# A 1 KB read at the head of a DMA queue, and a new order of the first loads, in a fused attention and gated-MLP kernel

## The chip, the cores and the metric

The kernel runs on one core of one Trainium2 chip. The metric is the device time of one execution in microseconds (us). All timed runs here count as fast (undisturbed) runs. One execution of each kernel was also profiled, and its trace is what the views below show. A trace has its own span, from the first to the last instruction, about 1.7 us shorter than the device time.

In the profile PE is TensorE's matmuls, PEld its weight loads, DVE the vector engine, ACT the scalar engine, POOL GpSimd and SP SyncE. A name with "q" (SPq, ACTq) is the engine's sequencer, which issues DMAs.

## The reference, cut to what matters

One token sequence of 2048 rows and 640 columns is layer-normalized and goes through two branches, which are added to the input.

```python
xn = _layernorm(x, axis=-1)
return x + _A_ref(xn, A_wqkv, A_w_phi, A_wo) + _B_ref(xn, B_w1, B_w3, B_w2)
# _A_ref: q, k, v = xn @ wqkv, 32 heads of 20; feature maps, linear attention; @ wo
# _B_ref: (silu(xn @ w1) * (xn @ w3)) @ w2, with 1536 hidden columns
```

All inputs are bf16. Only the opening matters here: row tiles of 128 rows of x are normalized, transposed on TensorE and multiplied by the value weights wv, the last 640 columns of wqkv. wv comes in five slices of 128 rows (160 KB each), because the product runs over 640 = 5 x 128.

## The kernel before

The opening issues ten small reads from two queues. SyncE (`nc.sync`) and ScalarE (`nc.scalar`) each work through their own queue in order.

```python
def load_wv(c, queue=nc.sync):
    queue.dma_start(out=wv[:, c, :], in_=wqkv3[:, c, 2 * D : 3 * D])

def setup():
    # ... tiles allocated
    nc.vector.memset(xg[0][:, 0, 320:328], 0.0)
    nc.sync.dma_start(out=xg[0][:, 0, 0:320], in_=x2[0:P, 0:320])       # row tile 0, first half
    nc.scalar.dma_start(out=xg[0][:, 0, 320:640], in_=x2[0:P, 320:640]) # second half; waits for the memset
    load_x(xg[0], 1, 1, 0)       # row tile 1
    load_wv(0, nc.scalar)
    load_wv(1)
    load_wv(2, nc.scalar)
    load_x(xg[0], 2, 1, 0)       # row tile 2
    load_wv(3, nc.scalar)
    load_wv(4)
    load_x(xg[0], 3, 1, 0)
    load_gu(0)                   # gate/up weights; more loads follow ...
```

Before any data is there, TensorE runs eight wide matmuls on constants (`dummies(8)`), which are meant to bring it to its full clock. For each of the first four row tiles: DVE takes statistics and centers, TensorE transposes ("T(t)", five matmuls of 128 columns), ACT or DVE copies the result, and TensorE runs ten matmuls of 320 columns with wv. T(2) is the transposes of tile 2. After the fourth tile the gate/up matmuls begin.

The kernel plans its order with a small scheduler, and later row tiles are fetched one by one:

```python
X_of[t] = plan.op("SP", 0.5, lambda: [load_x(xg[c], i, 1, c)], deps=[xg_of[c]], lat=2.5, after=30.0)
ln_stats(t, ("k", k))
```

DMAs take eight completion semaphores in turn, so a DMA waits until the one eight places before it has landed: in the trace of this kernel the first gate/up load is issued at 3.77 us, when row tile 1, eight places before, has landed at 3.76.

The softmax here doesn't subtract the row's maximum and nothing guards it: scores larger than these inputs give would overflow.

Of the kernel before, what the change touches and what calls it, by code (L numbers as in the profile page):

```python
# [8 lines left out]
P = 128  # L9
# [74 lines left out]
def kernel(  # L84
# [12 lines left out]
    nc = tc.nc  # L97
    bf = mybir.dt.bfloat16
# [6 lines left out]
    B_, S, D = A_x.shape  # L105
# [16 lines left out]
    x2 = A_x[0]  # L122
    out2 = out[0]

    consts = ctx.enter_context(tc.tile_pool(name="consts", bufs=1))
# [14 lines left out]
    xg = {}  # L140
# [23 lines left out]
    def load_x(dst, t0, n, k, queue=nc.sync):  # L164
        return queue.dma_start(
            out=dst[:, t0 : t0 + n, :],
            in_=x2[512 * k + t0 * P : 512 * k + (t0 + n) * P, :].rearrange("(t p) d -> p t d", p=P),
        )

    def load_gu(i):  # L170
        for w, src in zip((w1, w3), w13):
            nc.sync.dma_start(out=w[:, :, 384 * i : 384 * i + 384], in_=src[:, :, 384 * i : 384 * i + 384])
# [5 lines that stand above are left out]
        xg[0] = five.tile([P, 4, D], bf, name="xg", tag="five")  # L178
        xn[0] = five.tile([P, 4, D], bf, name="xn", tag="five")
        xg[1] = five.tile([P, 4, D], bf, name="xg", tag="five")  # L180
        nc.vector.memset(xg[0][:, 0, 320:328], 0.0)  # L181
        nc.sync.dma_start(out=xg[0][:, 0, 0:320], in_=x2[0:P, 0:320])
        nc.scalar.dma_start(out=xg[0][:, 0, 320:640], in_=x2[0:P, 320:640])  # L183
        load_x(xg[0], 1, 1, 0)
        load_wv(0, nc.scalar)
        load_wv(1)
        load_wv(2, nc.scalar)
        load_x(xg[0], 2, 1, 0)
        load_wv(3, nc.scalar)
        load_wv(4)  # L190
        load_x(xg[0], 3, 1, 0)
        load_gu(0)
        nc.sync.dma_start(out=wrow[:], in_=A_w_phi.rearrange("h j f -> (h j) f").rearrange("(g p) f -> p g f", p=P))
        load_gu(1)
        nc.sync.dma_start_transpose(out=wkT[:], in_=A_wqkv[:, D : 2 * D])
        load_x(xg[1], 0, 4, 1)
        load_gu(2)
        load_gu(3)
# [4 lines left out]
    band = consts.tile([P, 40], bf, name="band")  # L203
    band2 = consts.tile([P, 20], bf, name="band2")
    mask = consts.tile([P, NB, HB], bf, name="mask")
    rowsync = consts.tile([P, 1], bf, name="rowsync")
    hmask = consts.tile([P, NQ, GH], bf, name="hmask")

# [58 lines left out]
    plan = Plan(dict(bank=6, five=4, half=2, pair=4, phi=5, om=4, kv=2, th=3, gs=3, up=3, hT=3, big=3))  # L267
# [17 lines left out]
    xg_of = {0: plan.alloc("five", lambda: None)}  # L285
    xn_of = {0: plan.alloc("five", lambda: None)}
    xg_of[1] = plan.alloc("five", lambda: None)
    X_of = {}
# [3 lines left out]
    def ln_stats(t, k=None, parts=(0, 1)):  # L292
        c, i = divmod(t, 4)

        def fn():
            for h in parts:
                nc.vector.bn_stats(out=stats[:, t, h, :], in_=xg[c][:, i, h * 320 : (h + 1) * 320])  # L297
            if parts[-1] == 1:
                nc.vector.bn_aggr(out=mv[:, t, :], in_=stats[:, t, :, :])

        stats_of[t] = plan.op(
            "DVE", 0.44 * len(parts) + 0.21 * (parts[-1] == 1), fn, after=arrive[t] if t < 8 else 0.0,
            deps=[X_of.get(t), pin_of.get(k)],
        )
        return stats_of[t]
# [90 lines left out]
    def fetch(t, k):  # L396
        c, i = divmod(t, 4)
        if i == 0:

            def al():  # L400
                xg[c] = five.tile([P, 4, D], bf, name="xg", tag="five")

            xg_of[c] = plan.alloc("five", al)
        X_of[t] = plan.op("SP", 0.5, lambda: [load_x(xg[c], i, 1, c)], deps=[xg_of[c]], lat=2.5, after=30.0)
        ln_stats(t, ("k", k))

    def bank(shape, dt):
# [595 lines left out]
    for t in range(NST):  # L1003
        K(t)
        if t < 8:
            fetch(8 + t, t)
        if t == 4 or t == 8:
            LN(t // 4 + 1)
        fill(1.95 if t < 8 else 1.18)
        if t == 0:  # L1010
            LN(1, ("g", 0, gi - 1))
            plan.op("SP", 0.5, load_w2, deps=[XT_of[4]])
        if t >= 4:
            V(t)
        fill(1.95 if t < 8 else 1.18)
        if t >= 2:
            KV(t - 2)
        if 3 <= t < 8:
            for _ in range(2):
                wq_seq.pop(0)()  # L1020
                fill(0.4)
        if 8 <= t < 14:
            Q(t - 8)
# [48 lines left out]
    with tc.manual_schedule(engines={ET.PE, ET.DVE, ET.Activation, ET.Pool, ET.SP}):  # L1072
        setup()
        warm()
        constants()
        for o in plan.ops[:early]:
            o["fn"]()
        kv_constants()
        for o in order:
            if o["n"] >= early:  # L1080
                o["fn"]()
# [28 lines left out]
```

## Time and profile before

| | value | view |
|---|---|---|
| device time | 269.69 us, median of the first 6 runs (269.21 to 271.93) | timed runs |
| span of the trace | 267.9 us | page, first line |
| PE busy | 98% | page, part 1 |
| chain of waits | PE 96%, DMA 2% | page, part 4 |

These lines are of the page of the kernel before: span; busy time and share by engine; the chain that ended last, by engine.

```profile
span 267.9 us, 5109 instructions
...
PE 261.9 (98%) x1948; PEld 164.8 (62%) x1974; DVE 173.7 (65%) x334; ACT 122.3 (46%) x273; POOL 131.5 (49%) x118
...
PE 96%; DMA 2%; issue 1%; ACTq 0%; DVE 0%
```

TensorE is the bottleneck, and everything else counts only where it makes TensorE wait. To find where, cut the span. This windowed view of the kernel before shows the stretch from the first gate/up weight load to the last matmul (the columns are busy us and instruction counts by engine, then the granted clock, the DMA share and GB/s):

```profile
13.24:264.75 251.51, 250.12 (x1870) 157.90 (x1893) 164.92 (x306) 114.29 (x257) 126.83 (x92) 1.00 0.50 137
```

The last matmul starts 251.51 us after the first gate/up weight load, and TensorE is busy for all but 1.4 us of that. This rest is 26 holes of at most 0.06 us, and the page has 26 matmul records fewer than weight loads (1948 against 1974), so they look like lost records rather than waits. So the span falls into three parts: the opening (13.24 us), a block (251.51 us) and an end (267.85 - 264.75 = 3.10 us).

The opening in the chain of waits of the kernel before (start, length, what):

```profile
2.33 4.86 DMA wv<-in_A_wqkv_dram
7.18 0.04 issue
7.22 2.06 PE bank L461 x14
9.29 0.56 PE bank L416 x10
```

A read of wv issued at 2.33 us lands at 7.18, and from then on TensorE works through. In the timeline of the kernel before (start, length, engine, line, operation; in brackets the engine's idle time before it and what ended it) four groups show how tile 0 gets there, and the last wait:

```profile
2.82 0.89 DVE L297 BATCH_NORM_STATS2 stats<-xg 128x6 f32<-128x320 bf16 x2 [1.90 <-DMA xg<-in_A_x_dram]
...
4.33 0.57 PE L416 MATMUL bank<-ident,xn 128*128 128x128 bf16 x5
...
5.44 1.22 PE L461 MATMUL bank<-wv,xnT 128*128 128x320 bf16 x6 [0.36 <-ACT xnT L428]
...
7.22 2.06 PE L461 MATMUL bank<-wv,xnT 128*128 128x320 bf16 x14 [0.29 <-DMA wv<-in_A_wqkv_dram]
```

DVE starts when x arrives, the transposes run at 4.33, the first wv matmuls at 5.44. The view puts the last wait down to ACT, but the first of its two copies, all that these matmuls need to begin, had ended at 5.02; by the semaphores it was wv slice 0 that landed at 5.40.

### The profile page before, as it was taken

The page shows a single profiled execution, that of the slowest core. Times are in us where ns is not written, and L with a number is a line of the kernel's source. Part 1 is how long each engine was busy: PE and PEld are TensorE (multiplying, and loading weights), DVE is VectorE, ACT ScalarE, POOL GpSimd, SP SyncE. Part 2 cuts the span into 40 slices and gives each one's busy share as a digit, 9 for nine tenths or more (in the row PEclk, how much of TensorE's full clock was granted, in tenths as well). Part 3 has the DMA queues.
Part 4 walks back from the last instruction along what each step waited for, and adds up shares of the span by engine and source line. Part 5 has one row for each costly group of instructions (what it writes and reads, how often), then busy time and mean ns, then how long its engine had stood idle before and what let it go on. Part 6 is the DMA issues. An engine that isn't in the chain of part 4 may idle for free.

```text
span 267.9 us, 5109 instructions
## 1 busy us (share of the span) xinstructions
PE 261.9 (98%) x1948; PEld 164.8 (62%) x1974; DVE 173.7 (65%) x334; ACT 122.3 (46%) x273; POOL 131.5 (49%) x118
## 2 busy tenths in 40 slices
PE   8999999999999999999999999999999999999995
PEld 3645555555566666666555677765765665657774
DVE  5738798777665996876898748666367365443221
ACT  3857676656776676767545222234225213120000
POOL 3353679976557577699315715443542553112000
DMA  7999949200420027529295457395813937430401
GB/s 220 310 276 290 257 124 292 81 0 0 134 65 0 2 98 201 115 108 150 75 290 181 130 141 202 132 257 202 221 38 114 236 115 211 122 82 20 123 26 49
DMA packets 69528, 38.10 MB, mean 142 GB/s; under 512 B 49664, under 2 KB 67456, under 8 KB 69504
## 3 DMA queue, kind: packets, MB, share of 16 engines
q1 hardware_dynamic: 68784, 37.18, 50.6%
q10 hardware_dynamic: 720, 0.61, 0.7%
q8 instruction: 15, 0.25, 0.4%
q14 instruction: 9, 0.07, 0.1%
HBM read 12.81 MB, written 12.98 MB: 96 GB/s over the span
## 4 chain that ended last, share of the span: by engine, by line
PE 96%; DMA 2%; issue 1%; ACTq 0%; DVE 0%
PE bank L667 38%; PE bank L447 22%; PE bank L832 19%; PE bank L845 8%; PE rtbank L742 2%; PE bank L461 2%; DMA wv<-in_A_wqkv_dram 2%; PE bank L620 1%; PE kva L592 1%; PE kvb L592 1%; PE bank L416 0%; ACTq L175 0%; ACTq L183 0%; DVE res L859 0%; DVE xg L181 0%
## 5 line engine op out<-in xcount | busy, mean ns | idle before, releaser
L711 POOL TENSOR_TENSOR hT<-gs,up 128x512 bf16<-128x512 bf16 x43 | 49.7, 1156 | 81.4 <-ACT up L706 42.2
L667 PE MATMUL bank<-xnT,w_108 128*128 128x512 bf16 x235 | 59.2, 379 | 0.3
L667 PE MATMUL bank<-xnT,w_107 128*128 128x512 bf16 x219 | 58.2, 379 | 1.1
L832 PE MATMUL bank<-w_109,hT 128*128 128x320 bf16 (+2 forms) x396 | 55.1, 295 | 0.0
L447 PEld LDWEIGHTS <-xnT 128*128 128x128 bf16 x440 | 42.1, 98 | 17.6
L832 PEld LDWEIGHTS <-hT 128*128 128x128 bf16 x396 | 37.9, 98 | 15.2
L683 ACT ACTIVATE th<-bank 128x512 bf16<-128x512 f32 x48 | 28.7, 597 | 39.8 <-PE bank L667 39.1
L688 DVE SCALAR_TENSOR_TENSOR gs<-th,bank 128x512 bf16<-128x512 bf16 x48 | 32.8, 684 | 20.6 <-ACT th L683 20.0
L667 PEld LDWEIGHTS <-w_108 128*128 128x128 bf16 x240 | 23.5, 98 | 28.3
L859 DVE TENSOR_TENSOR res<-bank,xr 128x320 bf16<-128x320 f32 (+2 forms) x33 | 15.8, 478 | 38.6 <-PE bank L845 38.6
L706 ACT ACTIVATE up<-bank 128x512 bf16<-128x512 f32 x43 | 25.7, 597 | 22.5 <-PE bank L667 22.5
L667 PEld LDWEIGHTS <-w_107 128*128 128x128 bf16 x240 | 22.4, 97 | 20.9
L845 PE MATMUL bank<-wo,oT 128*128 128x320 bf16 (+2 forms) x165 | 24.7, 295 | 0.0
L447 PE MATMUL bank<-wkphi,xnT 128*128 128x320 bf16 x160 | 24.3, 299 | 0.0
L447 PE MATMUL bank<-wqphi,xnT 128*128 128x320 bf16 x160 | 24.3, 299 | 0.0
L845 PEld LDWEIGHTS <-oT 128*128 128x128 bf16 x165 | 15.8, 98 | 5.8
L447 PE MATMUL bank<-wv,xnT 128*128 128x320 bf16 x120 | 18.3, 299 | 0.0
L519 ACT ACTIVATE exp_128<-bank 128x320 bf16<-128x320 f32 x32 | 11.5, 435 | 13.6 <-PE bank L447 13.6
L519 ACT ACTIVATE exp_131<-bank 128x320 bf16<-128x320 f32 x32 | 11.5, 437 | 12.2 <-PE bank L447 12.2
L519 ACT ACTIVATE exp_129<-bank 128x320 bf16<-128x320 f32 x32 | 11.5, 435 | 10.7 <-PE bank L447 10.7
L519 ACT ACTIVATE exp_130<-bank 128x320 bf16<-128x320 f32 x32 | 11.5, 439 | 10.1 <-PE bank L447 10.1
L297 DVE BATCH_NORM_STATS2 stats<-xg 128x6 f32<-128x320 bf16 x32 | 13.7, 470 | 2.2 <-DMA xg<-in_A_x_dram 2.2
(141 smaller groups left out, 293.2 us busy)
## 6 DMA issues: line engine op xcount, KB each, us to landing
xr<-in_A_x_dram SPq DMA_DIRECT2D x4, 640.0 KB, 5.8
out_dram<-res SPq DMA_DIRECT2D x15, 160.0 KB, 1.9
w_107<-in_B_w_dram SPq DMA_DIRECT2D x4, 480.0 KB, 6.2
w_108<-in_B_w_dram SPq DMA_DIRECT2D x4, 480.0 KB, 6.7
w_109<-in_B_w_dram SPq DMA_DIRECT2D x1, 1920.0 KB, 8.7
xg<-in_A_x_dram SPq DMA_DIRECT2D x11, 160.0 KB, 3.6
wo<-in_A_wo_dram SPq DMA_DIRECT2D x1, 800.0 KB, 5.3
xg<-in_A_x_dram SPq DMA_DIRECT2D x1, 640.0 KB, 5.2
```

What stands on the lines that cost most here:

```text
L297: nc.vector.bn_stats(out=stats[:, t, h, :], in_=xg[c][:, i, h * 320 : (h + 1) * 320])
L447: nc.tensor.matmul(o["ps"][:], xnT[:, c, t * P : (t + 1) * P], w[:, c, 320 * half : 320 * half + 320], start=(c == 0), stop=(c == KD - 1),)
L461: nc.tensor.matmul(o[half]["ps"][:], xnT[:, c, t * P : (t + 1) * P], wv[:, c, 320 * half : 320 * half + 320], start=(c == 0), stop=(c == K ...
L519: nc.scalar.activation(out=box["e"][:, sgn, 16 * half : 16 * half + 16, :], in_=o["ps"][:].rearrange("p (h d) -> p h d", d=Dh), func=AF.Ex ...
L667: nc.tensor.matmul(o["ps"][:], w[:, k, fi * P : (fi + 1) * P], xs[:, k, :], start=(k == 0), stop=(k == KD - 1))
L683: nc.scalar.activation(out=box["th"][:], in_=og["ps"][:], func=AF.Tanh, scale=0.5)
L688: nc.vector.scalar_tensor_tensor(out=box["gs"][:], in0=box["th"][:], scalar=1.0, in1=og["ps"][:], op0=ALU.add, op1=ALU.mult)
L706: nc.scalar.activation(out=box["up"][:], in_=ou["ps"][:], func=AF.Copy, scale=0.5)
L711: lambda: nc.gpsimd.tensor_mul(out=hT[c][:, fi, :], in0=box["gs"][:], in1=box["up"][:]),
L832: nc.tensor.matmul(o["ps"][:], hT[c][:, fi, ti * P : (ti + 1) * P], w2[:, fi, lo:hi], start=(fi == 0), stop=False,)
L845: nc.tensor.matmul(o["ps"][:], oT[c][:, k, ti * P : (ti + 1) * P], wo_of[0][:, k, lo:hi], start=False, stop=(k == KD - 1),)
L859: nc.vector.tensor_tensor(out=box["res"][:, lo:hi], in0=o["ps"][:], in1=xr[c][:, ti, lo:hi], op=ALU.add)
```

## The change

The intent: the first read of a tensor may cost extra, so touch the weights once, early, with a read too small to cost bandwidth, while x is still on its way. Then spread x and wv over both queues so that TensorE finds both in time. A part loads the later row tiles in pairs.

```diff
-        nc.sync.dma_start(out=xg[0][:, 0, 0:320], in_=x2[0:P, 0:320])
-        nc.scalar.dma_start(out=xg[0][:, 0, 320:640], in_=x2[0:P, 320:640])
-        load_x(xg[0], 1, 1, 0)
-        load_wv(0, nc.scalar)
-        load_wv(1)
-        load_wv(2, nc.scalar)
-        load_x(xg[0], 2, 1, 0)
-        load_wv(3, nc.scalar)
+        nc.sync.dma_start(out=touch[:], in_=A_wqkv[0:P, 2 * D : 2 * D + 32].rearrange("(a b) d -> a b d", b=8)[:, 0, :])
+        nc.scalar.dma_start(out=xg[0][:, 0, 0:320], in_=x2[0:P, 0:320])
+        nc.sync.dma_start(out=xg[0][:, 0, 320:640], in_=x2[0:P, 320:640])
+        load_x(xg[0], 1, 1, 0, nc.scalar)
+        load_wv(0)
+        load_wv(1, nc.scalar)
+        load_wv(2)
+        load_x(xg[0], 2, 1, 0, nc.scalar)
+        load_wv(3)
         load_wv(4)
 # ...
+    touch = consts.tile([16, 32], bf, name="touch")
 # ... later row tiles, two a DMA
-        X_of[t] = plan.op("SP", 0.5, lambda: [load_x(xg[c], i, 1, c)], deps=[xg_of[c]], lat=2.5, after=30.0)
+        n = 2
+        if i % n == 0:
+            X_of[t] = plan.op("SP", 0.5, lambda: [load_x(xg[c], i, n, c)], deps=[xg_of[c]], lat=2.5, after=30.0)
+        else:
+            X_of[t] = X_of[t - 1]
```

The touch reads 16 rows of 32 numbers: 16 pieces of 64 bytes. Nothing ever reads `touch`.

## The prediction

> **What bounds the kernel now.** TensorE: the page gives PE 98% busy, the chain of waits is 96% PE. By the windowed busy times PE is never short of work from 13.8 us on (128.40 of 129.20 us up to 143 us; later gaps are missing matmul records), at granted clock 1.00. So about 254 us are a fixed block, and the change can win only where PE waits: the opening. In the timeline PE's first value-projection matmul (L461) starts at 5.44 us although its activations were copied by 5.0; two more stops end at 6.23 and 7.22. In the chain "DMA wv<-in_A_wqkv_dram" runs from 2.33 to 7.18 us, and PE pieces follow it nearly without a gap. By the semaphores, wv slices 0 to 4 land at 5.40, 5.59, 6.18, 7.18, 7.39 us; x tile 1 at 3.76, x tile 2 at 6.41 (the vector engine waits 0.30 us for it).
>
> **Why the weights are slow.** Between 3.2 and 4.4 us the DMA engines move about 271 KB where the later rate (136 to 150 KB per 0.4 us) would give about 420; there, packets of 1280 B that usually take 52 ns take 300 to 850. That is where wv is first read. About 0.45 us is lost, on some engines more: slice 0's first and last engine finish at 3.67 and 5.40. I take this as a first-access cost of the weight tensor (inferred, not shown).
>
> **What the change does.**
> - Adds one 16x32 read (1 KB) at the head of SyncE's queue, about 0.4 us of issue. The Trainium skill ("DMA: Bandwidth & Descriptors", section on why a DMA increments its semaphore by 16) says 16 rows use 16 engines: each meets the weights about 1.5 us earlier, while x is on its way.
> - Moves x tile 0's first half, x tiles 1 and 2 and slice 1 to ScalarE's queue; SyncE carries the other half (issued near 1.22, not 0.96) and the other slices. The same page ("Issuing engines are not separate DMA queues") says both queues share the engines, so this alone should save little.
> - Later x tiles come in pairs: four SyncE issues fewer near 27 to 30 us, off the path. Compute orders stay the same.
>
> **Sum.** Slices land 0.4 to 0.8 us earlier (slice 0 near 4.8, slice 3 near 6.5). PE's stops of 0.26, 0.25 and 0.4 us shrink, but T(2), tile 2's transposes, then waits for the vector chain: its input was ready at 8.57, it ran at 9.12. So about 0.55 us can be taken, and up to 0.28 more if x tile 2 lands earlier; T(3) follows. Against it: up to 0.2 us if the second half of x tile 0 lands after 3.27. PE stays full, so the gain of 0.5 to 0.6 us is passed on whole.
>
> **Prediction: 269.1 us** (before 269.69), 268.3 to 269.9 eight times in ten. Faster by over 2%: 0.01; within 2%: 0.98; slower by over 2%: 0.01.
>
> **What would show it.** Right: no "DMA wv" piece in the chain; slow packets gone from 3.2 to 4.4 us, a few near 2 us instead; the first gate/up matmul (L667) near 12.7 us instead of 13.24; everything later shifted as much. Wrong: slow packets still there; x tile 0 landing later because the touch blocks SyncE's ring; the vector chain holding T(2) at 9.1; new gaps in PE's later stretch.
>
> **What would make it wrong.** The slow packets belong to many pages rather than to the tensor, or the touch merely moves the delay in front of x. Then the time is 269.5 to 269.9.

## The result, and the profile after

The changed kernel took 269.82 us (median of 10 runs, 269.22 to 271.35) against 269.34 us (median of 20 runs, 269.02 to 271.93) for the kernel before. The ratio is 1.0017, with a 95% interval of 0.9994 to 1.0040: the same, leaning to slower. The time lies inside the predicted range, but the forecast gain of 0.6 us is not there. That it lies inside is luck: the range reached 0.2 us above the old time. The old time itself was drawn from six runs, three of them over 270 us; over all 20 it is 0.35 us lower.

The page of the kernel after:

```profile
span 267.6 us, 5106 instructions
...
PE 262.0 (98%) x1948; PEld 164.6 (62%) x1974; DVE 173.8 (65%) x334; ACT 122.3 (46%) x273; POOL 131.5 (49%) x118
...
PE 96%; DMA 2%; issue 1%; SPq 0%; DVE 0%
```

The chain of waits of the kernel after, its opening:

```profile
2.17 4.33 DMA wv<-in_A_wqkv_dram
6.50 0.04 issue
6.54 0.43 PE bank L467 x2
```

The timeline of the kernel after (its lines stand six further down than before):

```profile
0.80 0.40 SPq L182 DMA_DIRECT2D touch<-in_A_wqkv_dram  x1
...
1.26 0.40 SPq L184 DMA_DIRECT2D xg<-in_A_x_dram  x1
...
2.81 0.49 DVE L299 BATCH_NORM_STATS2 stats<-xg 128x6 f32<-128x320 bf16 x1 [1.88 <-DMA xg<-in_A_x_dram]
...
3.68 0.49 DVE L299 BATCH_NORM_STATS2 stats<-xg 128x6 f32<-128x320 bf16 x1 [0.38 <-DMA xg<-in_A_x_dram]
...
4.80 0.57 PE L422 MATMUL bank<-ident,xn 128*128 128x128 bf16 x5 [0.39 <-DVE xn L344]
...
5.60 0.72 PE L467 MATMUL bank<-wv,xnT 128*128 128x320 bf16 x4
...
6.54 0.43 PE L467 MATMUL bank<-wv,xnT 128*128 128x320 bf16 x2 [0.23 <-DMA wv<-in_A_wqkv_dram]
```

Before, DVE ran both statistics back to back from 2.82. Now there is a hole: the second half of tile 0 is issued at 1.26 and lands at 3.58 (before: issued 0.96, landed 3.00). The transposes stand at 4.80 instead of 4.33. The wv matmuls no longer wait for slice 0, which lands at 4.63 instead of 5.40, but they start at 5.60, later than before's 5.44. TensorE waits once more, 0.23 us until 6.54, for wv slice 2 (landed at 6.50). From the first transposes to the first gate/up weight load it takes 8.42 us instead of 8.91, but it starts 0.47 us later. So of the opening nothing is left but 0.02 us: that load starts at 13.22 instead of 13.24.

The span is nevertheless 0.2 us shorter (267.64 against 267.85). From the first gate/up load to the last matmul it is again 251.51 us; the end is 2.91 us instead of 3.10. So two things need a reason: why earlier weights bought nothing, and why the end is shorter.

### The profile page after: what moved, and what is told of

Read it like the earlier page. It is cut to its first block, busy times and chain, and to the rows that moved or that the text cites. A ratio compares the mean times of both kernels' runs of the same rounds, so it can differ in the third digit from the quotient of the medians.

```text
span 267.6 us, 5106 instructions
## 1 busy us (share of the span) xinstructions
PE 262.0 (98%) x1948; PEld 164.6 (62%) x1974; DVE 173.8 (65%) x334; ACT 122.3 (46%) x273; POOL 131.5 (49%) x118
## 4 chain that ended last, share of the span: by engine, by line
PE 96%; DMA 2%; issue 1%; SPq 0%; DVE 0%
PE bank L673 38%; PE bank L453 22%; PE bank L838 20%; PE bank L851 8%; PE bank L467 2%; PE rtbank L748 2%; DMA wv<-in_A_wqkv_dram 2%; PE bank L626 1%; PE kva L598 1%; PE kvb L598 1%; PE bank L422 1%; SPq L175 0%; SPq L182 0%; SPq L184 0%; DVE res L865 0%
## 5 line engine op out<-in xcount | busy, mean ns | idle before, releaser
L299 DVE BATCH_NORM_STATS2 stats<-xg 128x6 f32<-128x320 bf16 x32 | 13.8, 471 | 2.4 <-DMA xg<-in_A_x_dram 2.3
```

The lines of the kernel that those rows point to most:

```text
L299: nc.vector.bn_stats(out=stats[:, t, h, :], in_=xg[c][:, i, h * 320 : (h + 1) * 320])
```

## The experiments

**How the traces were compared.** In 13 of the 14 traces the block is 251.51 us long. A span is therefore the opening plus 251.51 us plus the end, and each timed run's opening can be worked out from its span (which is known to 0.1 us) and the end in that kernel's trace. Calling it "opening" below means that; "landing" is the time at which the last of a DMA's 16 semaphore updates arrives. The Trainium skill says in "DMA: Bandwidth & Descriptors" (section "Why a DMA increments its semaphore by 16 and not by 1") that a DMA runs on up to 16 engines that finish independently, each counting one. The traces agree: every load named here has 16 separate updates, except the touch of one row in e10.

**Theory after the result (A):** the touch does pay a first-access cost of the weights, but that cost now stands in front of x tile 0's second half. **Rival (B):** there is no such cost; the new queue order alone moves wv, and the touch is only in the way. Four runs on one chip were to tell them apart.

### e1_no_touch

```diff
-        nc.sync.dma_start(out=touch[:], in_=A_wqkv[...])
```

> The changed kernel without the touch: its queue order alone. Touch theory (the short read pays a first-access cost of the weight tensor, and the cost then stands in front of x tile 0's second half in SyncE's queue): packets of 300 us-thousandths and more return at 3.2 to 4.6 us, wv slice 0 lands at 5.1 to 5.5 us as before (4.63 with the touch), x tile 0's second half lands at 3.0 to 3.1 (3.58 with it), first transposes at 4.3 (4.80 with it). Rival (the new queue order brings wv early): slice 0 lands by 4.7 without any touch. Time within 0.3% of before either way.

("us-thousandths" is a slip for ns.) Measured: 269.11 us (median of 4) against 269.49 (7 runs of before); ratio 0.9991 (0.9976 to 1.0005). Without any touch slice 0 lands at 4.62 us, where it landed with it (4.63). Tile 0's second half is back at 3.00. The timeline of e1_no_touch:

```profile
2.79 0.89 DVE L298 BATCH_NORM_STATS2 stats<-xg 128x6 f32<-128x320 bf16 x2 [1.86 <-DMA xg<-in_A_x_dram]
...
4.29 0.73 PE L421 MATMUL bank<-ident,xn 128*128 128x128 bf16 x5
```

DVE has no hole, the transposes start at 4.29, the first gate/up load at 12.88. Packets longer than 250 ns are as frequent without the touch as with it: 19 between 1.5 and 7 us, against 15 after and 16 before. That speaks for B and against A.

### e2_touch_only

```diff
+        nc.sync.dma_start(out=touch[:], in_=A_wqkv[...])
         nc.sync.dma_start(out=xg[0][:, 0, 0:320], in_=x2[0:P, 0:320])
```

> The kernel before with the touch alone at the head of SyncE's queue, nothing moved. Touch theory: slice 0 lands at 4.5 to 4.9 us (5.40 before); x tile 0's first half, now behind the touch in SyncE's queue, lands at 3.4 to 3.7 (2.80 before) while the second half on ScalarE's queue stays at about 3.0; the vector engine starts its first statistics 0.6 to 0.9 us later than 2.82 and the first transposes stand at 4.9 to 5.2. Rival (queue order brings wv early, the touch does nothing): slice 0 at 5.2 to 5.5 and x tile 0 only 0.4 us later, the issue time.

Measured: 270.82 us (median of 4), ratio 1.0034 (1.0007 to 1.0060), the slowest kernel. Its one trace fits A's wording: tile 0's first half lands at 3.52 and slice 0 at 4.01. Slice 0 alone would have misled me again, see below; and here row tile 1 is issued behind slice 0 (1.72 us) and no longer before it (1.25), which may by itself let slice 0 land early. The trace shows a second thing that nobody expected, in the timeline of e2_touch_only:

```profile
8.58 2.69 PE L463 MATMUL bank<-wv,xnT 128*128 128x320 bf16 x13
```

Before needed 2.06 us for 14 of these matmuls. Here the first six start 0.27 us apart, the later ones 0.14, and the trace's first record of a fully granted clock is at 10.11 us; in nine of the ten other traces that have such a record it stands between 3.9 and 5.5 us, in e10_one_piece at 5.77. TensorE had idled for 0.65 us until 5.05 us. (It also waited 0.39 us for slice 2, whose last engine came at 6.99, 0.8 us behind the other fifteen.) The Trainium skill ("TensorE: Matmul & The Clock Gate", section "What's actually happening") says that the array starts at half clock and is released by a busy window of about 3.4 us that runs free of the kernel's start. This trace agrees with a release that slipped; no run shows the window itself.

### e3_touch_x

```diff
-        ... in_=A_wqkv[0:P, 2 * D : 2 * D + 32].rearrange(...)
+        ... in_=x2[0:P, 0:32].rearrange(...)
```

> The changed kernel with the same 16 short pieces read from x instead of the weights. Touch theory (cost belongs to the tensor first read, not to the place in the queue): x tile 0's second half lands at 3.2 to 3.4 us (3.58 with the weights touched; issue at 1.26 is the same), and wv slice 0 goes back to 5.1 to 5.5 with packets of 300 ns and more at 3.2 to 4.6 us. Rival (any short read at the head delays what follows it, and the order brings wv early): second half again at 3.5 to 3.6, slice 0 at 4.6 to 4.8.

Measured: 269.76 us (median of 4), ratio 1.0017 (0.9997 to 1.0036). A short read of x, which is read anyway at that moment, delays tile 0's second half too: it lands at 4.28 us although it was issued at 1.26 as in the kernel after. So the delay is not the weights' first access. This half of A is refuted. Slice 0 landed at 5.35; A expected 5.1 to 5.5, but e8_filler below, which touches the weights, shows the same pair (second half 4.25, slice 0 5.25). So the late slice says nothing about which tensor was touched.

### e4_touch_later

```diff
         nc.scalar.dma_start(out=xg[0][:, 0, 320:640], in_=x2[0:P, 320:640])
+        nc.sync.dma_start(out=touch[:], in_=A_wqkv[...])
         load_x(xg[0], 1, 1, 0)
```

> The kernel before with the touch second in SyncE's queue, behind x tile 0's first half; nothing else moved. Touch theory: both halves of x tile 0 land at 2.8 to 3.1 us, x tile 1 behind the touch at 4.0 to 4.4 (its reader begins at 4.42, so little is lost), slice 0 at 4.5 to 5.0; first transposes at 4.3, third tile's transposes up to 0.4 us earlier than 9.12, first gate/up matmul at 12.9 to 13.2 instead of 13.37, and the time 0.1 to 0.4 us below before's. Rival (vector chain or x tile 2 holds everything whatever wv does): first gate/up matmul at 13.3 to 13.4.

Measured: 269.98 us (median of 4), ratio 1.0033 (0.9996 to 1.0069). Both halves of tile 0 land in time (2.72 and 2.98) and slice 0 at 4.10, but what SyncE issues after the touch is late: tile 1 at 4.63, and tile 2 at 6.93 instead of 6.41. The gate/up matmuls start no earlier (weight load at 13.28). Moved back, the touch delays other reads instead.

### e5_b_again and the scatter of one trace

The kernel before, unchanged, one look.

> The kernel before once more, for the scatter of its opening from run to run. If wv slice 0's landing at 5.40 us is a property of its queue order, it lands at 5.2 to 5.6 again and the first gate/up matmul stands at 13.3 to 13.4; if it was one unlucky slow packet, slice 0 lands at 4.2 to 4.8 and the gate/up matmul at 12.9 to 13.2.

Measured: 269.26 us, state unknown (a single run). Slice 0 lands at 4.49, not 5.40. Nothing was changed. The 16 updates of slice 0 explain it:

```
slice 0, landing of each of the 16 engines, us
before, first trace   3.67 3.69 3.70 3.71 3.74 3.77 3.79 3.80 3.81 3.87 3.89 3.93 4.01 4.19 4.23 5.40
before, second trace  3.81 3.85 3.86 3.87 3.88 3.90 3.93 3.96 3.97 4.01 4.03 4.06 4.13 4.14 4.16 4.49
```

Fifteen engines had finished by 4.23 us in both. The 5.40 of the first trace was one straggling engine, not a property of the weights or of the queue order. The first-access idea began with it, and its second support falls as well: the slow stretch from 3.2 to 4.4 us is not there again. The last column of this windowed view is GB/s, from the kernel before and then from e5_b_again:

```profile
3.20:4.40 1.20, 1.16 (x5) 0.23 (x3) 1.13 (x5) 0.90 (x1) 0.22 (x2) 1.00 0.91 232
```

```profile
3.20:4.40 1.20, 1.13 (x5) 0.25 (x3) 1.13 (x6) 0.89 (x1) 0.22 (x2) 1.00 1.00 316
```

In e11_pairs_only, which has the same opening, it is 309 GB/s.

With it falls a part of B too. In the old order slice 0 lands at 4.49 (here) and 4.68 (e11), in the new order without touch at 4.62 (e1) and 5.05 (e7). That the new order brings slice 0 early is not shown either.

### e6_a_again and e7_no_touch_again

The kernel after unchanged, and e1 unchanged, five rounds each on the same chip.

> The changed kernel once more. New theory (the touch takes SyncE's first issue slot and holds up x tile 0's second half; it doesn't speed the weights): second half lands at 3.4 to 3.7 again, slice 0 at 4.5 to 4.8, first gate/up matmul 13.2 to 13.6. Clock theory (the late x leaves TensorE idle while its clock is being granted[...]): 3 to 5 of about 10 runs at 270 us or more, against 1 in 5 of the kernel before's.

> The changed kernel without the touch once more, with rounds enough for 0.1%. New theory: x tile 0's second half at 2.9 to 3.1 us, slice 0 at 4.4 to 4.9, first gate/up matmul at 12.9 to 13.1, time 0.1 to 0.4 us below before's; fewer than 1 run in 5 at 270 us or more. Rival (e1 was luck): first gate/up matmul at 13.3 to 13.4 and the time as before's.

Measured: e6_a_again 269.88 us (median of 6), ratio 1.0012 (0.9983 to 1.0040). e7_no_touch_again 268.85 us (median of 6), ratio 0.9976 (0.9951 to 1.0001). The two differ by the touch alone. Some of the expected landings were missed: e6's second half came at 3.82 and its slice 0 at 5.12, e7's slice 0 at 5.05 and its first gate/up matmul at 14.17.

The landings in the traces, in us (after and e6 have the touch):

| | before | e5 (before) | after | e6 (after) | e1 (no touch) | e7 (no touch) |
|---|---|---|---|---|---|---|
| tile 0, second half | 3.00 | 2.98 | 3.58 | 3.82 | 3.00 | 3.04 |
| wv slice 0 | 5.40 | 4.49 | 4.63 | 5.12 | 4.62 | 5.05 |
| wv slice 3 | 7.18 | 6.70 | 7.01 | 6.80 | 6.73 | 7.90 |
| x tile 2 | 6.41 | 6.25 | 6.71 | 6.58 | 6.53 | 7.69 |
| first gate/up load | 13.24 | 12.93 | 13.22 | 13.05 | 12.88 | 14.04 |

Two traces of one kernel differ by at most 0.24 us in the first row and by up to 1.2 us in the others. e7's profile caught that kernel's only run over 270 us (270.22 us; its other five are 268.70 to 268.91). Its timeline shows TensorE waiting for slice 1:

```profile
6.80 0.70 PE L466 MATMUL bank<-wv,xnT 128*128 128x320 bf16 x4 [1.22 <-DMA wv<-in_A_wqkv_dram]
```

Again it is one engine: slice 1's fifteenth update came at 5.89, the sixteenth at 6.76, and one update is about 0.9 us late in every load from there on. Such luck makes a single trace useless for a question of 0.3 us. The openings of all timed runs are better evidence:

| kernel | runs | median opening, us |
|---|---|---|
| before (rounds beside the experiments) | 29 | 13.1 |
| after and e6_a_again | 17 | 13.5 |
| e1_no_touch and e7_no_touch_again | 10 | 12.7 |

They are pooled from several sets of rounds and three chips, so they are less strict than the ratios, which compare within one set. On one chip, e6 against e7, the difference is largest: 13.8 against 12.6 us. What the order alone gains is not shown. The table suggests 0.3 to 0.4 us, the ratios' intervals reach 1, and e11_pairs_only below, whose opening is that of the kernel before, has a median opening of 12.9 us, as e1 has.

TensorE's waits tell which landing set the opening in a trace. These are windowed views from the first transposes to the first gate/up weight load, of e6_a_again, e3_touch_x and e8_filler, and then of the kernel after:

```profile
5.03:13.05 8.02, 7.96 (x72) 5.51 (x73) 6.92 (x22) 6.70 (x16) 1.50 (x2) 1.00 1.09 326
5.49:13.51 8.02, 7.99 (x73) 5.48 (x74) 6.92 (x22) 6.72 (x16) 0.95 (x2) 1.00 0.95 284
5.46:13.48 8.02, 8.00 (x75) 5.61 (x76) 6.91 (x22) 6.72 (x16) 0.90 (x2) 1.00 0.95 278
...
4.80:13.22 8.42, 8.12 (x73) 5.68 (x74) 7.02 (x22) 6.71 (x16) 2.00 (x6) 1.00 1.09 322
```

In the first three, where x tile 0's second half landed at 3.82, 4.28 and 4.25, TensorE works through, and the stretch is 8.02 us each time: the late x alone set these openings. In the kernel after (3.58) the same work could, by this measure, have been done at 4.80 + 8.02 = 12.82 us. It ended at 13.22 because TensorE also waited for slice 2, whose sixteenth update came at 6.50 and the fifteenth at 5.88. So that trace shows the touch's delay and a straggler at once, and the late x does not explain all of it.

Where does a touch of 16 pieces at SyncE's head show in every trace? In the first 1.3 us of DMA traffic. The last column of this windowed view is GB/s, from the kernel before, then after, then e1_no_touch:

```profile
1.50:2.80 1.30, 1.30 (x4) 0.46 (x3) 0.00 (x0) 0.00 (x0) 1.12 (x9) 1.00 0.72 204
```

```profile
1.50:2.80 1.30, 1.30 (x4) 0.44 (x3) 0.00 (x0) 0.11 (x1) 1.12 (x9) 1.00 0.52 102
```

```profile
1.50:2.80 1.30, 1.30 (x4) 0.46 (x3) 0.01 (x1) 0.15 (x1) 1.12 (x9) 1.00 0.74 184
```

e6_a_again has 102, e8_filler 125, e2_touch_only 133 and e3_touch_x 137; e5 and e7 have 187 and 192. The touch is 1 KB, but with it the engines move a half to three quarters as much while they should be filling up. At the later rate (349 GB/s between 4.4 and 7 us in the kernel before) the missing (184 - 102) GB/s x 1.3 us = 107 KB are an estimated 0.3 us.

### e8_filler

Half the changed kernel's runs (8 of 17, with e6) took 270 us or more, against 10 of 49 of before's. After e2 a late clock was suspected, since the touch leaves TensorE idle from 4.4 to 4.8 us. The pooled shares hide the chip, though: of before's runs it was 5 of 11 on the chip of e6 to e8, where e6 had 3 of 6, and 0 of 18 on the two other chips of the experiments.

```diff
-        dummies(8)
+        dummies(9)
-    plan.op("PE", 0.3, lambda: dummies(3, P))
+    plan.op("PE", 0.3, lambda: dummies(5, P))
```

> The changed kernel with its warm-up matmuls lengthened so that TensorE does not idle until x tile 0 is there: 9 wide ones for 8 and 5 narrow ones for 3. Clock theory: the touch's delay stays (second half at 3.4 to 3.7, first gate/up matmul 13.3 to 13.7), but the runs at 270 us and more become rare (at most 1 in 6 or so), so the median falls below e6_a_again's by 0.2 to 0.6 us although the opening is no shorter. Rival (the spread has nothing to do with TensorE's clock): the same share of slow runs, median equal or up to 0.2 us higher.

Measured: 269.58 us (median of 6), ratio 1.0004 (0.9973 to 1.0035). One of 6 runs is over 270, against 3 of 6 of e6's, and the median is 0.3 us below e6's. That is what the clock theory expected, but six runs can do this by chance, before itself had 5 of 11 over 270 in the same rounds, and x landed so late in this trace (4.25 us) that TensorE idled all the same. Inconclusive.

### e9_touch_pool

```diff
-        nc.sync.dma_start(out=touch[:], ...)
+        nc.gpsimd.dma_start(out=touch[:], ...)
```

> The changed kernel with the touch issued from GpSimd's queue instead of SyncE's, so that it takes no issue slot from x tile 0. If a touch of the weights helps at all once it stands in nobody's way (first-access theory), wv slices 0 and 1 land at 4.0 to 4.4 and 4.4 to 4.8 us, earlier than without a touch (4.62 and 4.98 in e1_no_touch), and the first gate/up matmul comes at 12.6 to 12.9. If the touch is pure cost (new theory): x tile 0's second half at 2.9 to 3.1, slices 0 and 1 at 4.5 to 5.1 on all but a straggling DMA engine, first gate/up matmul at 12.9 to 13.2, time as the kernel without touch, within 0.2 us.

Measured: 269.58 us (median of 4), ratio 1.0008 (0.9995 to 1.0021). Tile 0's second half is at 2.90 again, so SyncE's queue was indeed what the touch blocked. But the touch lands only at 5.05 us, and slices 0 and 1 at 5.22 and 5.46, no earlier than without it. Out of the way the touch still brings nothing; landing this late it is no full test of an early touch, though. GpSimd spends 0.74 us on it, and this is the one kernel whose block is longer, 251.78 us: TensorE loses some 0.3 us in all around 19 to 24 us, at the matmuls that use the transposed key weights wkT. The first of them starts at 19.76, when the DMA that brings wkT has landed (19.72); it was issued at 10.2 us instead of 9.1. I did not follow the rest.

### e10_one_piece

```diff
-        nc.sync.dma_start(out=touch[:], in_=A_wqkv[...])
+        nc.sync.dma_start(out=touch[0:1, :], in_=A_wqkv[0:1, 2 * D : 2 * D + 32])
```

> The changed kernel with a touch of one piece instead of 16: the same issue slot at SyncE's head, but only one of the 16 DMA engines reads. Slot theory (the touch pushes the issue of x tile 0's second half from 0.95 to about 1.26 us, behind x tile 1 on the other queue, with which it then shares the engines): second half lands at 3.4 to 3.9 as with 16 pieces. Read theory (what the 16 engines read ahead holds it up): second half lands at 3.2 to 3.35, that is 3.0 plus the 0.3 of issue.

Measured: 269.61 us (median of 4), ratio 1.0012 (0.9997 to 1.0026). Tile 0's second half lands at 3.22 us, as the read theory wanted: by this one trace 0.2 us of the 0.6 to 0.8 us are the issue slot, and the rest comes only when all 16 engines read. The timeline of e10_one_piece:

```profile
2.76 1.05 DVE L299 BATCH_NORM_STATS2 stats<-xg 128x6 f32<-128x320 bf16 x2 [1.84 <-DMA xg<-in_A_x_dram]
```

DVE's hole is nearly gone. Yet the median opening (13.5 us) is that of the kernel after. Every later load of SyncE is still issued 0.2 to 0.4 us later than in e1, and slice 3 and tile 2 land at 7.15 and 6.93, each through one late engine (the other fifteen by 6.50 and 6.21). So the slot may also cost something further down the queue; how much each part costs in the time is not settled by one trace and four runs.

### e11_pairs_only

The kernel before with only the last part of the diff, two row tiles a DMA.

> The kernel before with only the later x tiles loaded in pairs (four DMAs fewer), nothing changed in the opening. End theory (the last store's semaphore is no longer third but sixth or seventh of those that SyncE goes through at the end): from the last matmul's start to the end of the span 2.88 to 2.97 us instead of 3.10; first gate/up matmul where before's traces have it, 13.0 to 13.4; time 0.1 to 0.2 us below before's. Rival (the pairs do nothing): the end part 3.08 to 3.14 again.

Measured: 269.11 us (median of 4) against 269.40 (11), ratio 0.9992 (0.9979 to 1.0005). The end is 2.95 us long instead of 3.10, as expected. SyncE's last instructions in the traces show why:

```
before: last store lands on semaphore 104 at 266.83; SyncE then passes waits at 266.89, 266.95, 267.01
after:  last store lands on semaphore 109 at 266.79; SyncE then passes a wait at 266.80 and is done
```

At its end SyncE passes five wait instructions, some 0.06 us apart, that take the semaphores in a fixed order: 105 first, 104 in the second, 108 in the fourth, 109 in the fifth. Before, the last store used 104, and three more wait instructions followed. Four DMAs fewer and one touch more move it to the fifth. The end is 3.14 to 3.16 us when four follow (semaphore 105; e2, e4), 3.10 to 3.11 with three (104), 2.95 with one (108; e1, e7, e11) and 2.89 to 2.92 with none (109). So in the traces the pairs shorten the end by 0.15 us, by nothing that they were meant for. The timed ratio agrees, but its interval reaches 1.

### e12_no_memset

e1 without the small memset that the second half of tile 0 waits for, as an attempt at something better still.

```diff
-        nc.vector.memset(xg[0][:, 0, 320:328], 0.0)
```

> The changed kernel without the touch and without the vector engine's small memset that SyncE's first read waits for: an attempt at a version better than both. If an earlier start of the reads is worth something: x tile 0's second half issued at 0.80 instead of 0.95, landing at 2.8 to 2.95, all later landings 0.1 earlier, first gate/up matmul at 12.85 to 13.0, median 268.6 to 268.9. Rival (the landings of wv slice 3 and x tile 2 are set by the engines' rate, not by the issue): as e7_no_touch_again, 268.85 within 0.15 us.

Measured: 269.35 us (median of 6), ratio 1.0000 (0.9986 to 1.0014). A miss. Both halves are now issued at 0.79 and 0.80 and land at 3.22 and 3.06, where e1 had 2.76 and 3.00. DVE, which needs the first half first, starts at 3.24. In this one trace the two reads start together, and the one needed first is 0.46 us late. The memset, odd as it looks, staggers them; that this is why e12 is no better than before was not tested.

**The best version** is the change without its touch (e1 and e7): medians of 269.11 and 268.85 us, against 269.49 and 269.48 for before in the same rounds. The intervals reach 1.0005 and 1.0001, so it is likely but not proven that it beats before. How much of that is the order is open: e11_pairs_only, with before's opening, also has a median of 269.11 us. Against the kernel after, e7's 268.85 compares with e6's 269.88 on the same chip.

## Why the prediction was right or wrong

- **What bounds the kernel: right.** The block after the first gate/up load is 251.51 us before and after. Only the opening and, unforeseen, the end moved.
- **"I take this as a first-access cost of the weight tensor": wrong, and the step that failed.** The touch itself, the first read of the weights in the execution, landed 1.50 us after its issue (1.66 in e6); the equally short read of x in e3 took 1.86. That short read of x did the same harm. Slow packets are as many without a touch (19) as with it (15), and those between 3.2 and 4.4 us, which were to vanish, are 6 with it (after, e6), 4 and 5 without (e1, e7), and 9 and 4 in the two traces of before. The 5.40 us and the slow stretch from 3.2 to 4.4 us that the prediction built on belonged to one trace; the same kernel gave 4.49 us, and 316 GB/s instead of 232, in the next.
- **"Slices land 0.4 to 0.8 us earlier (slice 0 near 4.8, slice 3 near 6.5)": right in number for slice 0 alone, and no effect of the change.** Slice 0 landed at 4.63, slice 3 at 7.01. Without the touch they land at 4.62 and 6.73 (e1), and in the unchanged kernel's second trace at 4.49 and 6.70 (e5).
- **"Both queues share the engines, so this alone should save little": not refuted.** It is what the Trainium skill says ("DMA: Bandwidth & Descriptors", section "Issuing engines are not separate DMA queues"), and the traces do not contradict it: between 4.4 and 7 us the engines move 333 GB/s in e1 and 349 in the kernel before. The order without the touch is ahead of before by about 0.3 us in the median opening, but no experiment shows that the order did it (e11).
- **"Against it: up to 0.2 us if the second half of x tile 0 lands after 3.27": right in kind, far too small.** It landed at 3.58 and 3.82 (4.25 in e8), and in the first two the transposes started 0.47 and 0.70 us later than 4.33. The median opening of the 17 runs with the touch is about 0.8 us longer than that of the 10 without.
- **"T(2), tile 2's transposes, then waits for the vector chain": not what held it.** T(2) ran at 9.10 instead of 9.12. Its input was ready at 8.87, but TensorE, which had waited for slice 2 until 6.54, was busy with earlier matmuls until then. The stops did shrink, by 0.49 us from the first transposes on; the late start of 0.47 us ate that.
- **"The gain of 0.5 to 0.6 us is passed on whole": the passing on was right.** Any change of the opening appears in the span one for one; there was no gain to pass.
- **The pairs "off the path": wrong by 0.15 us.** They changed which semaphore the last store uses (e11).
- **The list of what would make it wrong came nearest:** "the touch merely moves the delay in front of x", with 269.5 to 269.9 us. It measured 269.82. What the list did not doubt was that there was a delay to move.

As a sum, from before to after: the end -0.2 us, the median opening about +0.4 us; together +0.2 us, against +0.3 and +0.5 us in the ratios 1.0012 and 1.0017.

What stays open: how a 1 KB read on all 16 engines holds up the next DMA by more than its issue slot; whether the new order gains anything; and whether the many runs over 270 us come from straggling DMA engines (seen in e7's and e2's traces of such runs), from a late clock (seen in e2's trace, and perhaps in one of e4's timed runs, 271.90 us with a mean granted clock of 0.993) or from both.

## What to carry to other kernels

A DMA lands when its last engine does. Before you explain a late landing, look at all 16 updates and at a second trace, because one straggler looks like a slow tensor. A read that nobody waits for does not belong at the head of a queue, however small: here it held up the read behind it by 0.2 us (one piece) to 1.3 us (16 pieces). And a difference between two traces is not an effect until the unchanged kernel has been traced twice. If a long block of the trace repeats to 0.01 us, subtract it, and let all the timed runs, not one trace, speak about the rest.

## What the Trainium skill lacked or had wrong

- "DMA: Bandwidth & Descriptors", section "Issuing engines are not separate DMA queues", calls the issue time usually small beside the DMA. Here one issue takes 0.40 us, and a 1 KB read ahead in the same queue made an 80 KB read land 0.58 and 0.82 us later in two traces, at 3.58 and 3.82 us instead of 3.00.
- The same page tells of DMA engines that are usually slower and suspects a cause in GpSimd's DMA path. It has nothing on one engine falling behind in single runs of loads issued from SyncE and ScalarE: 5.40 us against 4.23 for the other fifteen in one trace, 0.9 us behind for seven loads in a row in another. (The trace does not name the engine.)
- No page that I read tells that the place of the last store's semaphore among those that SyncE checks at the end costs time: 2.89 to 3.16 us of end, depending on how many of five wait instructions follow.
- "TensorE: Matmul & The Clock Gate" agrees with the one late clock seen (10.11 us in e2_touch_only). The windowed view shows a granted clock of 1.00 there, before the first record, although the matmuls started 0.27 us apart instead of 0.14; trust the spacing.
